# A gated mix of linear attention and an S4D convolution: running sums by accumulating transfers in pairs of rows, one to two iterations apart

## The chip, the cores and the metric

The kernel runs on one core of a Trainium2 chip. The metric is device time in microseconds (us): the median of several runs. The core has five engines with a program each, which run in order and meet at semaphores: TensorE (PE, its weight loads listed as PEld), VectorE (DVE), ScalarE (ACT), GpSimd (POOL) and SyncE (SP). SP and POOL also issue transfers (DMA); POOL issues those that accumulate into their destination. All data are 32-bit floats; matmuls run on a rounded high part and a low part of each operand so as to keep precision.

## The reference, cut to what matters

```python
g = sigmoid((x * gate_w).sum(-1, keepdims=True))           # x: 1 x 2048 x 448
a = attention(x, wqkv, wo)
b = s4d(x, log_A_real, A_imag, C_real, C_imag, log_dt, D_skip)
return g * a + (1 - g) * b

def attention(x, wqkv, wo):                                # 16 heads of 28
    q, k, v = split(x @ wqkv)
    phi = lambda t: where(t > 0, t + 1, exp(t)) + 1e-6
    kv  = einsum("bhsd,bhse->bhde", phi(k), v)
    z   = einsum("bhsd->bhd", phi(k))
    o   = einsum("bhqd,bhde->bhqe", phi(q), kv) / (einsum("bhqd,bhd->bhq", phi(q), z) + 1e-6)
    return merge(o) @ wo

def s4d(u, ...):                                           # K from A, C and dt, then a causal convolution
    return irfft(rfft(u, 2L) * rfft(K, 2L))[:L] + u * D_skip
```

## The kernel before

The 2048 rows of `x` are cut into NC = 16 chunks of 128 rows (one row on each partition), and the chunks into four groups of G = 4. Row `p` of a group's partition dimension holds four consecutive positions, one in each of its four chunks.

For parameters like these the convolution's kernel is constant to the precision needed apart from its first tap, so that the convolution is a running sum of `x` along the sequence, times a factor per channel (`near`). A second routine, `general_conv`, stands behind a test of the parameters and does not run here. The running sum of a group is made in three stages:

- Inside a partition over its four rows: `group_load` (L422, a transfer that SP issues) brings the four chunks into the group's `homes[g]`, then two transfers that accumulate, both `running` (L427, issued by POOL), add shifted rows. Step 1 adds rows 0 to 2, read from HBM, to rows 1 to 3; step 2 adds rows 0 and 1 of the result to rows 2 and 3, inside SBUF. Step 2 may not start before step 1 has landed, and POOL waits for that where step 2 stands in its program.
- Across partitions: `group_split` takes the group's last row into a high part (ACT, L431) and a low part (POOL, L242, tile `sums`), and `group_heads` multiplies both by a triangle of ones on TensorE (L438).
- `convolve` (L443 and L444, DVE) adds the heads to two of the four rows at a time and multiplies by `near`. Then `group_add` (L450) is another accumulating transfer, from `homes[g]` into `y`, and the last row's values go to `u` (L447, SP).

The main loop (L503 to L562) runs over chunks 2 to 13. One pass c projects K of chunk c + 1 (`project`, 11 matmuls, L340), projects q of chunk c (11 matmuls) and accumulates the outer product of `xn` and `phi(k)` of chunk c into four PSUM banks (`do_g`, 11 matmuls, L415). `split_t` prepares the turned chunk c + 2 for TensorE: ACT copies the high part and POOL subtracts it for the low part (`xt`, L246 and L242); `split_n` does so for the plain chunk (`xn`, L252 and L242) and also starts `y` with `x * D_skip` (L258, POOL). `k_feature`, `k_high` and `k_low` make `phi(k)` on ACT and DVE (L366 to L378), `q_post` makes `phi(q)` (L386 to L393) and keeps it in `pq`. The q projection has one PSUM bank, so that q of the next chunk waits until L393 has read the last one.

The order on each engine is that of the code: the schedule is written out by hand, as positions in the loop. `group_load` of group g stands in pass 2g + 2, step 1 at that pass's end, step 2 in the middle of pass 2g + 3 (behind `split_t`), `group_split` in pass 2g + 4, `group_heads` in pass 2g + 5, and `convolve` in passes 2g + 6 and 2g + 7.

The homes are `spare`, half of the weights' tile `wvo` (whose real contents, `wo`, come in pass 10), the last four chunks of `pq` (whose real contents come from pass 12 on; the first loads put the S4D parameters there, and `s4d_prepare` reads them in the first passes), and `spare` again for the last group.

Behind the loop the matrices of attention and output projection are multiplied together, and for each chunk `norm_a` to `norm_d` (POOL and DVE) divide q by its denominator, `turn` transposes it and `attend` (11 matmuls, L660) makes the output rows, which `final_b` mixes with `y` and sends out.

## Time and profile before

| | |
|---|---|
| median of 3 runs | 199.99 us (198.42 to 200.40) |
| the profiled execution | 200.24 us |
| its span, first to last instruction | 198.5 us |
| mean granted TensorE clock | 0.953 |
| busy: PE / PEld / DVE / ACT / POOL | 170.5 / 149.9 / 134.3 / 106.1 / 120.0 us |
| transfers: SP's queue / POOL's queue | 21.81 MB / 8.26 MB |
| mean rate of the transfers | 153 GB/s |

The profile is of one execution; its times are counted from the start of its span. In a row of the instructions in order of time stand: start, length, engine, line, operation, output and inputs, shapes, how many like it were merged, and in brackets the idle time of the engine ahead of it with what ended that. A matmul's length reaches over the start of the next, since they are pipelined. Instructions on POOL that follow a transfer's issue are likewise shown with lengths that overlap the next. A row of waits gives the engine, the waiting tile and its line, what it waited for, the total in us, the number of times and the longest. The main loop lies between about 22 and 138 us.

### The profile page before, as it was taken

To read this page: it belongs to the slowest core of one execution; us is meant where nothing else is said; L and a number is where in the kernel's file an instruction comes from. 1 tells how busy PE (TensorE), PEld (TensorE's weight loads), DVE (VectorE), ACT (ScalarE), POOL (GpSimd) and SP (SyncE) were. 2 spreads that over 40 slices of the span, in tenths; PEclk is the share of its full clock that TensorE was granted. 3 is DMA by queue.
4 is the path that set the end of the run, shared out by engine and by line. 5 is a ranking of instruction groups with operands and counts; after the bars stand their busy time and mean duration, and the time that the engine had idled before them with its cause. 6 is when DMAs were issued, how large, how long until landed. Compare 5 with 4: busy or idle time off the path is not lost.

```text
span 198.5 us, 2704 instructions
## 1 busy us (share of the span) xinstructions
PE 170.5 (86%) x852; PEld 149.9 (76%) x852; DVE 134.3 (68%) x232; ACT 106.1 (53%) x241; POOL 120.0 (60%) x128
## 2 busy tenths in 40 slices
PE   7999999860499879952997988997999999999991
PEld 2798999750498769931896867995897999999990
DVE  0758566710498167997561888878789798997550
ACT  3787788700526195317453645974746466455531
POOL 5246588205970991880519946798597799774200
PEclk9999999997579999996699999999999999999998
DMA  6999683995978409896588799109003122222212
GB/s 199 417 291 266 186 299 117 301 242 131 289 234 146 92 2 139 198 185 225 105 209 160 139 257 225 59 0 185 1 1 63 48 93 93 92 94 96 93 65 82
DMA packets 12186, 30.37 MB, mean 153 GB/s; under 512 B 1549, under 2 KB 7898, under 8 KB 12170
## 3 DMA queue, kind: packets, MB, share of 16 engines
q1 hardware_dynamic: 9274, 21.81, 33.5%
q0 software_dynamic: 2752, 8.26, 23.2%
q8 instruction: 7, 0.11, 0.3%
q10 hardware_dynamic: 144, 0.11, 0.2%
q14 instruction: 9, 0.07, 0.1%
HBM read 20.68 MB, written 3.67 MB: 123 GB/s over the span
## 4 chain that ended last, share of the span: by engine, by line
PE 38%; DMA 28%; DVE 10%; POOL 9%; ACT 8%; issue 5%; ACTq 0%; POOLq 0%; SPq 0%
PE a L660 18%; DMA spare<-in 13%; DMA wvo<-in 5%; DMA pq<-in 4%; PE g L415 4%; PE tr L634 4%; POOL y L258 3%; PE v L340 3%; DMA y<-spare 3%; POOL xn L242 3%; PE q L264 2%; PE q L340 2%; DVE pq L444 2%; DVE spare L444 2%; DMA spare<-spare 2%
## 5 line engine op out<-in xcount | busy, mean ns | idle before, releaser
L340 PE MATMUL q<-wqh,xt 128*128 128x450 f32 x120 | 29.9, 388 | 8.2 <-DVE pq L393 8.2
L660 PE MATMUL a<-wk,th 128*128 128x448 f32 (+1 forms) x170 | 36.7, 361 | 0.1
L415 PE MATMUL g<-pkh,xn 128*128 128x448 f32 x112 | 35.9, 366 | 0.0
L340 PEld LDWEIGHTS q<-wqh,xt 128*128 128x128 f32 x120 | 23.6, 202 | 11.8 <-DVE pq L393 9.7
L660 PEld LDWEIGHTS a<-wk,th 128*128 128x128 f32 x170 | 29.4, 189 | 2.4 <-ACT th L645 0.4
L340 PE MATMUL k<-wk,xt 128*128 128x448 f32 x77 | 20.4, 404 | 11.7 <-POOL xt L242 11.7
L242 POOL TENSOR_TENSOR xt<-xr,xt 128x512 fp32r<-128x512 f32 x14 | 23.7, 1696 | 8.6 <-ACT xt L246 8.6
L340 PEld LDWEIGHTS k<-wk,xt 128*128 128x128 f32 x77 | 15.4, 207 | 14.8 <-POOL xt L242 13.2
L242 POOL TENSOR_TENSOR xn<-xr,xn 128x448 fp32r<-128x448 f32 x16 | 23.5, 1471 | 4.5 <-ACT xn L252 4.4
L415 PE MATMUL g<-pkl,xn 128*128 128x448 f32 x64 | 23.5, 367 | 0.0
L415 PEld LDWEIGHTS g<-pkh,xn 128*128 128x128 f32 x112 | 21.2, 189 | 2.3
L340 PE MATMUL v<-wk,xt 128*128 128x448 f32 x99 | 21.6, 364 | 0.9 <-POOL xt L242 0.9
L258 POOL TENSOR_TENSOR y<-xr,rows 128x448 f32<-128x448 f32 x16 | 22.3, 1393 | 0.0
L572 POOL TENSOR_TENSOR prod<-pq,zb 128x448 f32<-128x448 f32 x16 | 18.6, 1172 | 3.6 <-ACT zb L694 2.6
L340 PEld LDWEIGHTS v<-wk,xt 128*128 128x128 f32 x99 | 18.5, 188 | 2.5 <-POOL xt L242 1.3
L597 POOL TENSOR_TENSOR pn<-pq,den 128x336 f32<-128x336 f32 x16 | 12.3, 768 | 7.5 <-ACT den L586 5.3
L665 DVE SCALAR_TENSOR_TENSOR ot<-y,og,a 128x448 f32<-128x448 f32 (+1 forms) x17 | 10.7, 629 | 5.5 <-PE a L660 5.5
L378 DVE SCALAR_TENSOR_TENSOR pkl<-v,pkh 128x448 fp32r<-128x448 f32 x9 | 5.6, 619 | 13.1 <-ACT pkh L372 13.0
L642 DVE TENSOR_TENSOR th<-tr,th 128x512 fp32r<-128x512 f32 x16 | 11.0, 691 | 2.7 <-ACT th L641 2.1
L378 DVE SCALAR_TENSOR_TENSOR zb<-v,zb 128x448 f32<-128x448 f32 x9 | 5.6, 620 | 10.2 <-ACT pkh L372 10.2
L415 PEld LDWEIGHTS g<-pkl,xn 128*128 128x128 f32 x64 | 11.3, 177 | 1.3 <-DVE pkl L378 0.2
L340 PE MATMUL q<-wql,xt 128*128 128x450 f32 x45 | 12.2, 379 | 0.0
(171 smaller groups left out, 334.6 us busy)
## 6 DMA issues: line engine op xcount, KB each, us to landing
xr<-in SPq DMA_DIRECT2D x15, 512.0 KB, 5.0
out<-ot SPq DMA_DIRECT2D x15, 224.0 KB, 1.9
pq<-in SPq DMA_DIRECT2D x4, 448.0 KB, 13.0
spare<-in SPq DMA_DIRECT2D x2, 896.0 KB
wvo<-in SPq DMA_DIRECT2D x2, 896.0 KB, 11.9
y<-spare POOLq DMA_DIRECT2D x2, 896.0 KB, 6.6
spare<-in POOLq DMA_DIRECT2D x2, 672.0 KB, 10.4
y<-in SPq DMA_DIRECT2D x2, 480.0 KB, 3.8
```

Source lines behind the costliest of these rows:

```text
L242: eng.tensor_tensor(out=o, in0=r, in1=h.bitcast(F32), op=ALU.subtract)
L258: POOL.tensor_tensor(out=y[:, c], in0=plain[c][:, :D], in1=dsk, op=ALU.mult)
L340: PE.matmul(o[:, :n], lhsT=a, rhs=b, start=run.n == 1, stop=not seq)
L378: DVE.scalar_tensor_tensor(out=o, in0=pk, scalar=1e-6, in1=a, op0=ALU.add, op1=op)
L415: PE.matmul(g[i][:a.shape[1], :D], lhsT=a, rhs=b, start=c == 0 and n == 0, stop=c == NC - 1 and n == len(seq) - 1)
L444: DVE.tensor_tensor(out=a, in0=a, in1=near[:, None, :].to_broadcast(full), op=ALU.mult)
L572: POOL.tensor_tensor(out=pd[c], in0=pq[:, c], in1=zb, op=ALU.mult)
L597: POOL.tensor_tensor(out=n[:, :3, :DJ].rearrange("p j (h d) -> p j h d", h=4), in0=a, in1=r[:, :H - 4].rearrange("p (j h) -> p j h", j=3)[ ...
L634: PE.transpose(o[:, j * P:(j + 1) * P], n[:, j], ident)
L642: DVE.tensor_tensor(out=l, in0=ov, in1=h.bitcast(F32), op=ALU.subtract)
L660: PE.matmul(a[:, lo:hi], lhsT=u_, rhs=w_[:, lo:hi], start=n == 0, stop=n == 10)
L665: DVE.scalar_tensor_tensor(out=ot[:, lo:hi], in0=y[:, c, lo:hi], scalar=og[:, c:c + 1], in1=a[:, lo:hi], op0=ALU.mult, op1=ALU.add)
```

## The change

Only the first stage of the running sum and its places change, with the homes.

`running` becomes two steps of another form, both inside SBUF and both over two rows. `running_a` adds row 0 to row 1 and row 2 to row 3 in one transfer. `running_b` adds row 1 to rows 2 and 3, with row 1 read twice. Step b has to wait until a has landed; a has to wait until the group's load has landed. The rows read again from HBM in the old step 1 (672 KB for each group) are no longer read; both new steps move 448 KB.

A table, `pieces_at`, gives the pass in which each step is issued, always behind `split_t`. Loads are in passes 2, 4, 5 and 7 (before: 2, 4, 6, 8), steps a in 3, 5, 6 and 8, steps b in 4, 6, 8 and 10, splits in 5, 7, 9 and 11 (before: 4, 6, 8, 10). Heads, `convolve` and `group_add` keep their passes.

A new tile `room` is the home of the third group. The first group's home is now `wvo`, the second's the end of `pq`, the fourth's `spare`, so that none is used twice. `room` is as large as the tiles `prod` (three slots) and `pn` (two slots) of the part behind the loop, which now live in it; `zl` moves to the slot of `sums`.

```diff
+    room = const.tile([P, 2 * NAT + 3 * D], F32, name="room")
...
-    homes = (spare, wvo[:, 1], pq[:, NC - G:], spare)
+    homes = (wvo[:, 1], pq[:, NC - G:], room[:, :G * D].rearrange("p (r d) -> p r d", r=G), spare)
...
-    def running(g, step):
+    def running_a(g):
         w = homes[g]
-        src = xin[g * G:(g + 1) * G - 1, :, NAT:LO].rearrange("r p d -> p r d") if step == 1 else w[:, :G - step]
-        POOL.dma_start(out=w[:, step:], in_=src, accum_op=ALU.add)
+        POOL.dma_start(out=w[:, 1::2], in_=w[:, 0::2], accum_op=ALU.add)
+
+    def running_b(g):
+        w = homes[g]
+        POOL.dma_start(out=w[:, 2:], in_=w[:, 1:2].to_broadcast([P, 2, D]), accum_op=ALU.add)
...
+    pieces_at = {3: [(running_a, 0)], 4: [(running_b, 0)], 5: [(running_a, 1)], 6: [(running_b, 1), (running_a, 2)],
+                 8: [(running_b, 2), (running_a, 3)], 10: [(running_b, 3)]}
...
-        if c in (2, 4, 6, 8):
-            group_load(c // 2 - 1)
+        if c in (2, 4, 5, 7):
+            group_load(c // 2 - (c < 5))
...
-        if c in (3, 5, 7, 9):
-            running(c // 2 - 1, 2)
+        for f, k in pieces_at.get(c, ()):
+            f(k)
...
-        if c in (4, 6, 8, 10):
+        if c in (5, 7, 9, 11):
             group_split(c // 2 - 2)
...
-        if c in (2, 4, 6, 8):
-            running(c // 2 - 1, 1)
...
-        pd[c] = tp.tile([P, D], F32, name="prod", tag="pk", bufs=3)
+        pd[c] = room[:, 2 * NAT + c % 3 * D:][:, :D]
...
-        n = pn[c] = tp.tile([P, J, P], F32, name="pn", tag="pn")
+        n = pn[c] = room[:, c % 2 * NAT:][:, :NAT].rearrange("p (j t) -> p j t", j=J)
...
-    zl = tp.tile([P, D], F32R, name="zl", tag="pk", bufs=3)
+    zl = tp.tile([P, D], F32R, name="zl", tag="v0", bufs=1)
```

How POOL's program changes is seen around the first group. Before, from the end of pass 2 (L427 is a step of the running sum, `y<-xr,rows` is `y`'s start, `xt`, `xn` and `sums` are low parts):

```order
L427 DMA spare<-in 128x3x448
L242 TENSOR_TENSOR xt<-xr,xt 128x512
L427 DMA spare<-spare 128x896
L258 TENSOR_TENSOR y<-xr,rows 128x448
L242 TENSOR_TENSOR xn<-xr,xn 128x448
L258 TENSOR_TENSOR y<-xr,rows 128x448
L242 TENSOR_TENSOR xt<-xr,xt 128x512
L242 TENSOR_TENSOR sums<-spare,sums 128x448
```

After, from pass 3 on, where the lines are counted by the new file (L427 is step a, L431 step b, L243 and L259 are the former L242 and L258):

```order
L243 TENSOR_TENSOR xt<-xr,xt 128x512
L427 DMA wvo<-wvo 128x2x448
L259 TENSOR_TENSOR y<-xr,rows 128x448
L243 TENSOR_TENSOR xn<-xr,xn 128x448
L259 TENSOR_TENSOR y<-xr,rows 128x448
L243 TENSOR_TENSOR xt<-xr,xt 128x512
L431 DMA wvo<-wvo 128x2x448
L243 TENSOR_TENSOR xn<-xr,xn 128x448
L259 TENSOR_TENSOR y<-xr,rows 128x448
L243 TENSOR_TENSOR xt<-xr,xt 128x512
L427 DMA pq<-pq 128x2x448
L243 TENSOR_TENSOR sums<-wvo,sums 128x448
```

One `xt` stood between the two steps of the first group; now there are four low parts and starts of `y` between them, and the first step of the second group stands ahead of the first group's `sums`.

On SP, behind the load of the weights into `wvo`, the loads of chunks (`xr`), of groups and the rows of `u` stood so before (L422 is a group's load, L447 a row of `u`):

```order
L422 DMA wvo<-in 128x4x448
L206 DMA xr<-in 128x1024 x2
L422 DMA pq<-in 128x4x448
L206 DMA xr<-in 128x1024
L447 DMA u<-spare 1x16x28 x2
L535 DMA okr<-oks 1x112x1
L206 DMA xr<-in 128x1024
L422 DMA spare<-in 128x4x448
```

and now (L423 is a group's load, L451 a row of `u`):

```order
L423 DMA pq<-in 128x4x448
L207 DMA xr<-in 128x1024
L423 DMA room<-in 128x4x448
L207 DMA xr<-in 128x1024 x2
L423 DMA spare<-in 128x4x448
L451 DMA u<-wvo 1x16x28 x2
L541 DMA okr<-oks 1x112x1
L207 DMA xr<-in 128x1024 x2
```

All group loads now stand ahead of the first rows of `u`; before, the last one stood behind them.

## The prediction

> **What bounds the kernel now.** I read the waits first, then TensorE's instructions in order of time with the idle time ahead of them, then POOL and DVE over the same stretch. In the waits (engine, tile and line, what it waited for, us in total, times, longest) the transfers of the running sums stand out:
>
> ```profile
> POOL spare L427 <- DMA spare<-in: 22.5, 3, 10.5
> ACT sums L431 <- DMA wvo<-wvo: 4.0, 1, 4.0
> POOL wvo L427 <- DMA wvo<-in: 6.6, 1, 6.6
> POOL pq L427 <- DMA pq<-in: 4.8, 1, 4.8
> ```
>
> POOL stands still for 22.5 + 6.6 + 4.8 = 33.9 us because L427 issues the second step of a group's running sum and must first see the first step landed. POOL works in order, so everything behind L427 waits too, among it the low halves `xt` (L242) that TensorE's next K projection needs. What that costs is read on TensorE (start, length, operation, count, idle time before it and its releaser):
>
> ```profile
> 36.27 2.27 PE L340 MATMUL v<-wk,xt 128*128 128x448 f32 x10 [0.88 <-POOL xt L242]
> 42.79 0.36 PE L340 MATMUL k<-wk,xt 128*128 128x448 f32 x1
> 52.18 4.10 PE L340 MATMUL k<-wk,xt 128*128 128x448 f32 x10 [9.03 <-POOL xt L242]
> 56.08 2.17 PE L340 MATMUL q<-wqh,xt 128*128 128x450 f32 x8
> ...
> 69.48 2.27 PE L340 MATMUL k<-wk,xt 128*128 128x448 f32 x10 [0.63 <-POOL xt L242]
> 72.84 1.89 PE L340 MATMUL q<-wqh,xt 128*128 128x450 f32 x8 [1.08 <-DVE pq L393]
> ...
> 85.46 2.27 PE L340 MATMUL k<-wk,xt 128*128 128x448 f32 x10 [0.68 <-POOL xt L242]
> 93.21 3.37 PE L340 MATMUL q<-wqh,xt 128*128 128x450 f32 x8 [5.47 <-DVE pq L393]
> 96.38 1.33 PE L340 MATMUL q<-wql,xt 128*128 128x450 f32 x3
> ...
> 108.72 2.28 PE L340 MATMUL k<-wk,xt 128*128 128x448 f32 x10 [1.34 <-POOL xt L242]
> ...
> 119.94 1.89 PE L340 MATMUL q<-wqh,xt 128*128 128x450 f32 x8 [1.68 <-DVE pq L393]
> ...
> 124.48 2.37 PE L340 MATMUL k<-wk,xt 128*128 128x448 f32 x11
> 126.68 1.77 PE L340 MATMUL q<-wqh,xt 128*128 128x450 f32 x8
> 128.29 0.76 PE L340 MATMUL q<-wql,xt 128*128 128x450 f32 x3
> ...
> 131.09 2.37 PE L340 MATMUL v<-wk,xt 128*128 128x448 f32 x11
> ```
>
> The gaps between 35 and 120 us sum to 0.88 + 9.03 + 0.63 + 1.08 + 0.68 + 5.47 + 1.34 + 1.68 = 20.8 us. Behind the two long ones the same matmuls run slower: 10 in 4.10 instead of 2.27 us and 8 in 2.17 instead of 1.77 after the first (2.2 us lost), 8 in 3.37 and 3 in 1.33 instead of 1.77 and 0.76 after the second (2.2 us). The page's row of the granted clock dips at just these places:
>
> ```profile
> PEclk9999999997579999996699999999999999999998
> ```
>
> The Trainium skill (TensorE: Matmul & The Clock Gate, Part 1) says that about one idle window of some 3.4 us takes the clock to half until the array has been busy for as long; the trace agrees, since gaps of 5.47 and 9.03 us were followed by slow matmuls and gaps up to 1.68 us were not.
>
> So 20.8 + 4.4 = 25.2 us of this stretch is TensorE waiting or running slow. Undisturbed, an iteration takes 131.09 - 124.48 = 6.61 us on it. The stretch behind the loop has nothing to give: TensorE is busy for all of 160 to 180 us.
>
> ```profile
> 160.00:180.00 20.00, 20.00 (x115) 18.48 (x114) 18.24 (x45) 11.76 (x30) 17.42 (x25) 1.00 0.23 88
> ```
>
> **The waits that go.** POOL's record around the first and the third group, with a quiet `y` and `xt` ahead for their price:
>
> ```profile
> 25.55 1.16 POOL L258 TENSOR_TENSOR y<-xr,rows 128x448 f32<-128x448 f32 x1
> 26.67 1.29 POOL L242 TENSOR_TENSOR xt<-xr,xt 128x512 fp32r<-128x512 f32 x1
> ...
> 33.46 1.44 POOL L427 DMA_DIRECT2D spare<-in  x1
> 34.42 1.79 POOL L242 TENSOR_TENSOR xt<-xr,xt 128x512 fp32r<-128x512 f32 x1
> ...
> 80.07 0.91 POOL L427 DMA_DIRECT2D pq<-pq  x1 [4.77 <-DMA pq<-in]
> ...
> 86.96 1.74 POOL L242 TENSOR_TENSOR sums<-pq,sums 128x448 fp32r<-128x448 f32 x1
> ```
>
> Before, the dependent second step stands one `xt` behind the first. Afterwards `running_a` and `running_b` of a group are one iteration apart (two for groups 2 and 3), so about 6.6 us of other work lies between issue and wait. Their landing times, from the view of transfers (KB, us from issue to landing; the 12.9 is the first group's, in the window 20 to 34 us):
>
> ```profile
> spare<-spare POOLq DMA_DIRECT2D x2, 448.0 KB, 4.3
> pq<-pq POOLq DMA_DIRECT2D x1, 448.0 KB, 4.8
> pq<-in POOLq DMA_DIRECT2D x1, 672.0 KB, 7.4
> spare<-in POOLq DMA_DIRECT2D x1, 672.0 KB, 12.9
> ```
>
> Both new steps move 448 KB inside SBUF. The trace has no such transfer in rows of 448 elements, only contiguous ones of that size (4.3 and 4.8 us) and three-row ones from HBM (7.4 with little beside it, 12.9 amid loads). I take 5 to 7, nearest the first kind, with 4.3 and 12.9 as ends. All these waits on L427, and the five gaps that name `xt` (0.88 + 9.03 + 0.63 + 0.68 + 1.34 = 12.6 us), go, with 2.2 us of slow clock. POOL issues eight such transfers before and after; each holds it for at most the 0.96 us between 33.46 and 34.42, so that is no change. The fourth group also no longer waits for the first one's `y` addition to free its home.
>
> The other three gaps, 1.08 + 5.47 + 1.68 = 8.2 us and 2.2 of slow clock, come through DVE. The 1.08 follows ACT's wait of 4.0 us for the second step (L431 on `wvo`) and goes with it. The long ones are these:
>
> ```profile
> 80.80 8.87 DVE L444 TENSOR_TENSOR wvo<-wvo,rows 128x896 f32<-128x896 f32 x1
> 111.93 4.46 DVE L444 TENSOR_TENSOR pq<-pq,rows 128x896 f32<-128x896 f32 x1
> 120.92 2.08 DVE L444 TENSOR_TENSOR spare<-spare,rows 128x896 f32<-128x896 f32 x1
> ```
>
> The 8.87 us one ends at 89.67, 0.97 us after POOL's unbroken run from 80.07 ended at 86.96 + 1.74 = 88.70: it got through only when POOL stopped. That run is POOL catching up after its wait. 8.87 led to the gap of 5.47, 4.46 to that of 1.68, and 2.08 to none. With POOL no longer late, the long runs shorten, but they do not vanish: iterations 6, 8 and 10 now put one or two transfers between `xt` and `xn`, in the very place where L444 asks for its turn. Two transfers, `xn` and `y` are 2 x 0.96 + 2 x 1.16 = 4.2 us, about what made the 4.46. I charge two of the three with 1.25 us each, 2.5 in all; ends are 0 and, for one of the old size, 5.47 + 2.2.
>
> The Trainium skill (SBUF — State Buffer, Who interferes with whom) says that a DVE instruction with two SBUF inputs shares a read port with GpSimd, locked for one whole instruction. By that rule alone L444 would lose one POOL instruction, 1.3 us or so, the 2.5 us would be nought and the forecast 177.5 instead of 180.0; here it lost a whole run of 8.6 us, so the measurement decides.
>
> **What the change adds.** `group_split` moves one iteration later, into the same iteration as `group_heads`. In POOL's order shown with the change, `sums` (the low half that the heads need) stood five instructions behind the second step, with an iteration of TensorE still ahead of the heads. Now another group's step a, which waits for that group's load, stands ahead of `sums`, and the heads follow in the same iteration.
>
> The first group is the tight one. POOL's `xt` moves up to 33.46, step a issues at 33.46 + 1.29 = 34.8; with 0.96 for it, 3 x 1.16 and 1.29 for the work behind, step b follows at 40.5, or when a has landed (34.8 + 5 to 7), so at 40.5 to 42. Landed at 45.5 to 49. Then ACT's copy and POOL's low half, from these:
>
> ```profile
> 51.17 0.57 ACT L431 CAST sums<-spare 128x448 fp32r<-128x448 f32 x1 [11.43 <-DMA spare<-spare]
> 51.81 1.42 POOL L242 TENSOR_TENSOR sums<-spare,sums 128x448 fp32r<-128x448 f32 x1
> ```
>
> 0.57 + 1.42 = 2.0, so ready at 47.5 to 51. TensorE starts that iteration at 42.79 - 0.88 = 41.9 and comes to the heads at its end, 6.61 later, at 48.5. Wait: 0 to 2.5 us; I take 1.5. If b lands only after 12.9 us it is 8.4.
>
> For groups 1 to 3 the time from step b to the split is a period plus ACT's way from its `xt` copy to the end of the second K exponential, less `xt` on POOL:
>
> ```profile
> 126.68 0.62 ACT L246 CAST xt<-xr 128x512 fp32r<-128x512 f32 x1
> ...
> 128.29 0.58 ACT L367 ACTIVATE e<-e 128x448 f32<-128x448 f32 x1
> ```
>
> 6.61 + (128.87 - 126.68) - 0.62 - 1.29 = 6.9 us against a landing of 5 to 7, or 7.4: nearly hidden. I charge 1.0 for the three together (0 to 18). Without that cover the whole landing would fall on ACT, and `pkh` and the `q` exponentials are queued behind it.
>
> On SP the loads of groups 1 to 3 (L422) change home and place, as its order shows: all three now stand ahead of the first `u` rows. The one into `pq` overwrites the parameters that the S4D preparation reads, the last time here:
>
> ```profile
> 37.85 0.69 DVE L298 SCALAR_TENSOR_TENSOR y<-pq 112x512 f32<-112x512 f32 x1
> ```
>
> It goes out at 38.5 at the earliest; its step a comes behind step b of the first group, after 40.5, an `xn`, a `y` and an `xt`, so at 45 or later. Behind it on SP is an `x` load that was itself held back before, by POOL's wait. No cost.
>
> The new tile `room` also carries `prod` and `pn` in the tail, with as many slots as before (three and two); its group's `y` addition is issued in iteration 11, far ahead of the first `norm_a`. `zl` shares a slot with `sums`, last read in iteration 11. Both cost nothing unless that addition landed over ten us late.
>
> **The sum.** 25.2 - 1.5 - 2.5 - 1.0 = 20.2 us off the span of 198.5, so 178.3. The profiled execution took 200.24 us, 1.74 outside its span, and stands 0.25 over the median of 199.99. 178.3 + 1.74 = 180.0; the 0.25 is within the spread of the runs, so I forecast 180.0.
>
> **Rivals.** *POOL's runs still shut out L444.* For it: the 8.87, and more transfers in mid-iteration. Against: POOL's run then was a backlog from a wait that goes. One hit of the old size in place of a charge of 1.25: 180.0 + 7.6 - 1.25 = 186.4; two: 192.8. Chance 0.15.
>
> *The loads crowd each other.* With a home for each group, loads that waited for an earlier group now go out early, beside the `x` loads. Two 896 KB loads issued together took
>
> ```profile
> wvo<-in SPq DMA_DIRECT2D x2, 896.0 KB, 11.9
> ```
>
> A step a that waits 5 us longer for its load, with `sums` behind it, would hold the heads for up to that: 185. Against it: in SP's order each `x` load still stands ahead of the next group's load. Chance 0.12.
>
> *Slower: the chain load, a, b, split, heads is too short.* Should every b land in L us, TensorE waits L - 4.5 for the first group (42 + L + 2.0 against 48.5) and at most L - 6.9 for each other, with 2.2 of slow clock behind each. 4L - 25.2 + 8.8 passes the 25.2 gained by 2 us at L = 10.9. At 12.9 it is 35.2, thus 198.5 - 25.2 + 35.2 + 1.74 = 210.2. For it: that 12.9 was measured. Against: its source was HBM and it was 672 KB; those inside SBUF took 4.3 to 4.8. Chance 0.04.
>
> *It does not do what it says:* the waits only move to L431, with the same sum, 200. The iteration between speaks against it. Chance 0.03.
>
> **The numbers.** The forecast has 0.66, with its own range from the floor, 198.5 - 25.2 + 1.74 = 175.0, to 184 (heads at 2.5, 1.5 from the others and 5 from L444). The range 175.5 to 188 adds the crowded loads and one old-size hit, leaving out the rest, under 0.2. About 1% is what a measurement of this kernel can tell from no change. Faster by over 1%: 0.66 + 0.15 + 0.12 = 0.93; same 0.03; slower 0.04.
>
> **What would show it.** Right: no wait of POOL on a first step over 3 us, TensorE's gaps before 115 us under 6 us together and no dip in its clock, iterations near 6.7 us. The heads of the first group should show a gap of 0 to 2.5 behind `sums`. L444 at 4 to 5 us in two of iterations 6, 8 and 10 bears out the 2.5; at 8 the first rival. It would be wrong if step b landed in over 9 us, or ACT stood before `sums` for over 3 us in each group.

## The result, and the profile after

| | before | after |
|---|---|---|
| median of 4 runs | 199.22 us (198.42 to 200.40) | 184.48 us (181.43 to 186.07) |
| the profiled execution | 200.24 us | 185.1 us |
| its span | 198.5 us | 183.2 us |
| mean granted TensorE clock | 0.953 | 0.987 |
| transfers, all queues | 30.37 MB | 29.45 MB |

The ratio is 0.916, with a 95% interval from 0.902 to 0.931. It is lower than the ratio of the two medians, because a ratio leaves out runs more than 1.5% above the fastest of the same kernel: here two of the four of the changed kernel, among them the profiled one, and further down, among others, one of 276 us (the homes alone) and one of 580 us (the operand in PSUM). In a second series the same kernel took 186.17 us (185.46 to 186.5) against 199.33, a ratio of 0.934 (0.931 to 0.938), and its profile shows the same two longest gaps on TensorE. The change makes the kernel about 7 to 8% faster; the forecast was 180.0 us.

The lines of the changed file are L427 for step a, L431 for step b, L435 for ACT's copy into `sums`, L243 for POOL's low parts (`sums`, `xt`, `xn`), L442 for the heads, L448 for the second instruction of `convolve` and L454 for `group_add`.

The page's row of the granted clock of after has one dip in the main loop, where before had two deep ones:

```profile
PEclk9999999999996999999999999999999999999998
```

TensorE of after in order of time, with the idle time ahead of an instruction in brackets. These are all the gaps between 35 and 120 us, with the projection behind the longest one:

```profile
45.75 1.85 PE L341 MATMUL q<-wqh,xt 128*128 128x450 f32 x8 [1.77 <-DVE pq L360]
...
56.06 1.12 PE L442 MATMUL v<-sums,tri 128*128 128x448 f32 x2 [5.23 <-ACT rows L321]
56.97 3.32 PE L341 MATMUL v<-wk,xt 128*128 128x448 f32 x11
...
74.71 1.88 PE L341 MATMUL q<-wqh,xt 128*128 128x450 f32 x8 [0.70 <-DVE pq L394]
...
86.26 0.47 PE L442 MATMUL v<-sums,tri 128*128 128x448 f32 x1 [0.59 <-ACT sums L435]
87.47 0.47 PE L442 MATMUL v<-sums,tri 128*128 128x448 f32 x1 [0.75 <-POOL sums L243]
...
98.21 1.87 PE L341 MATMUL q<-wqh,xt 128*128 128x450 f32 x8 [1.04 <-DVE pq L394]
...
103.62 0.47 PE L442 MATMUL v<-sums,tri 128*128 128x448 f32 x1 [0.93 <-POOL sums L243]
```

Before, five of eight gaps named `xt`, and none does now. The gaps sum to 1.77 + 5.23 + 0.70 + 0.59 + 0.75 + 1.04 + 0.93 = 11.0 us. Behind the longest, the 11 matmuls of `v` take 3.32 us instead of the usual 2.37 and the two of the heads 1.12 us instead of 0.67 (the row is shown with the run without steps), so the slow clock takes another 1.4. Together 12.4 us, against 25.2 before.

The releaser named at 56.06, `rows` (L321), is a copy that stands in ACT's program behind the one into `sums` (L435) and was late with it. The waits show for what:

```profile
ACT sums L435 <- DMA wvo<-wvo: 8.1, 1, 8.1
...
ACT sums L435 <- DMA room<-room: 2.6, 1, 2.6
...
POOL wvo L431 <- DMA wvo<-wvo: 2.1, 1, 2.1
```

POOL's waits on a first step have shrunk from 33.9 us to 2.1. In their place ACT stands 8.1 us before the copy into the first group's `sums`, until that group's step b has landed. The chain of waits gives the two steps of that group (start, us from issue to landing):

```profile
34.71 7.74 DMA wvo<-wvo
42.75 11.27 DMA wvo<-wvo
```

The gap of 1.77 us has another origin. DVE and POOL of after around the first group's step a:

```profile
35.66 5.59 DVE L299 SCALAR_TENSOR_TENSOR y<-pq 112x512 f32<-112x512 f32 x1
...
41.29 0.69 DVE L299 SCALAR_TENSOR_TENSOR y<-pq 112x512 f32<-112x512 f32 x1
...
66.20 4.96 DVE L448 TENSOR_TENSOR wvo<-wvo,rows 128x896 f32<-128x896 f32 x1
...
90.52 4.13 DVE L448 TENSOR_TENSOR room<-room,rows 128x896 f32<-128x896 f32 x1
```

```profile
34.71 1.33 POOL L427 DMA_DIRECT2D wvo<-wvo  x1
35.63 1.61 POOL L259 TENSOR_TENSOR y<-xr,rows 128x448 f32<-128x448 f32 x1
37.03 1.32 POOL L243 TENSOR_TENSOR xn<-xr,xn 128x448 fp32r<-128x448 f32 x1
38.14 1.30 POOL L259 TENSOR_TENSOR y<-xr,rows 128x448 f32<-128x448 f32 x1
39.25 1.44 POOL L243 TENSOR_TENSOR xt<-xr,xt 128x512 fp32r<-128x512 f32 x1
42.75 1.21 POOL L431 DMA_DIRECT2D wvo<-wvo  x1 [2.06 <-DMA wvo<-wvo]
```

The S4D preparation's reading at L299 takes 0.69 us, and 5.59 us right behind the issue of step a. It ends at 41.25, 0.56 us after POOL's unbroken run from 34.71 ended at 39.25 + 1.44 = 40.69. That is the picture of L444 in the profile of before, at a place where it had not been. The K feature, on which the next q projection waits through L360, comes behind it on DVE. The second series shows the same at L299 (5.58 us). For L448 only the 4.1 us of pass 10 returned there; in pass 7, where POOL had paused for 0.41 us just before, it took 1.15.

### The profile page after: what moved, and what is told of

Same layout as the page of the kernel before. It is cut to its first block, busy times and chain, and to the rows that moved or that the text cites. A ratio compares the mean times of both kernels' runs of the same rounds, so it can differ in the third digit from the quotient of the medians.

```text
span 183.2 us, 2706 instructions
## 1 busy us (share of the span) xinstructions
PE 166.5 (91%) x852; PEld 147.8 (81%) x852; DVE 130.4 (71%) x232; ACT 105.9 (58%) x241; POOL 123.2 (67%) x128
## 2 busy tenths in 40 slices
DMA packets 12186, 29.45 MB, mean 161 GB/s; under 512 B 1549, under 2 KB 8410, under 8 KB 12170
## 3 DMA queue, kind: packets, MB, share of 16 engines
HBM read 17.93 MB, written 3.67 MB: 118 GB/s over the span
## 4 chain that ended last, share of the span: by engine, by line
PE 51%; DMA 20%; DVE 8%; ACT 8%; POOL 6%; issue 2%; SPq 1%; ACTq 0%; DVEq 0%; POOLq 0%
PE a L664 20%; DMA wvo<-wvo 10%; PE g L416 8%; PE v L341 7%; PE q L341 6%; DMA room<-room 5%; PE tr L638 4%; PE k L341 3%; DVE wvo L448 3%; DMA wvo<-in 3%; DVE room L448 2%; POOL xt L243 2%; DMA y<-in 2%; POOL y L259 2%; POOL xn L243 2%
## 5 line engine op out<-in xcount | busy, mean ns | idle before, releaser
L341 PE MATMUL q<-wqh,xt 128*128 128x450 f32 x120 | 27.8, 368 | 3.5 <-DVE pq L360 1.8
L243 POOL TENSOR_TENSOR xt<-xr,xt 128x512 fp32r<-128x512 f32 x14 | 21.2, 1515 | 14.2 <-ACT xt L247 14.2
L243 POOL TENSOR_TENSOR xn<-xr,xn 128x448 fp32r<-128x448 f32 x16 | 23.9, 1492 | 5.7 <-ACT xn L253 3.9
L341 PEld LDWEIGHTS q<-wqh,xt 128*128 128x128 f32 x120 | 22.3, 188 | 6.2 <-DVE pq L394 2.5
L259 POOL TENSOR_TENSOR y<-xr,rows 128x448 f32<-128x448 f32 x16 | 21.8, 1365 | 0.0
L576 POOL TENSOR_TENSOR room<-pq,zb 128x448 f32<-128x448 f32 x16 | 18.6, 1168 | 3.6 <-issue 2.6
L341 PEld LDWEIGHTS v<-wk,xt 128*128 128x128 f32 x99 | 19.5, 197 | 1.5
L341 PE MATMUL k<-wk,xt 128*128 128x448 f32 x77 | 17.4, 368 | 0.1
L601 POOL TENSOR_TENSOR room<-pq,den 128x336 f32<-128x336 f32 x16 | 12.2, 763 | 7.4 <-ACT den L590 4.4
L341 PEld LDWEIGHTS k<-wk,xt 128*128 128x128 f32 x77 | 14.3, 187 | 1.8 <-ACT wk L464 0.4
L645 ACT CAST th<-tr 128x512 fp32r<-128x512 f32 x16 | 9.4, 588 | 4.6 <-PE tr L638 4.4
L373 ACT ACTIVATE pkh<-v 128x448 fp32r<-128x448 f32 x9 | 4.9, 543 | 12.3 <-DVE v L369 12.3
```

The lines of the kernel that those rows point to most:

```text
L243: eng.tensor_tensor(out=o, in0=r, in1=h.bitcast(F32), op=ALU.subtract)
L259: POOL.tensor_tensor(out=y[:, c], in0=plain[c][:, :D], in1=dsk, op=ALU.mult)
L341: PE.matmul(o[:, :n], lhsT=a, rhs=b, start=run.n == 1, stop=not seq)
L576: POOL.tensor_tensor(out=pd[c], in0=pq[:, c], in1=zb, op=ALU.mult)
L601: POOL.tensor_tensor(out=n[:, :3, :DJ].rearrange("p j (h d) -> p j h d", h=4), in0=a, in1=r[:, :H - 4].rearrange("p (j h) -> p j h", j=3)[ ...
L645: ACT.copy(h, ov)
```

## The experiments

The theory that the prediction leaves standing: the gain comes from the passes in which the steps are issued, because POOL no longer waits for its own first step. What is missing of it has two causes. A transfer that POOL issues ahead of other work shuts out DVE until POOL pauses (the shut-out), and a step lands late beside other transfers (the crowding). The rivals: that the new form or the homes bring the gain; that a step is slow whatever is beside it; that the rest of the idle time has nothing to do with the steps.

### What brings the gain

The changed kernel once more, unaltered, as a baseline of its own series:

> The changed kernel unaltered, as the measure for the kernels timed beside it. Both theories: between 181 and 186 us, as in its first timing.

It took 186.17 us, with gaps of 1.77 us ahead of the q projection and 5.04 us ahead of the first heads.

Then the old form of the steps in the new passes and homes:

```diff
     def running_a(g):
         w = homes[g]
-        POOL.dma_start(out=w[:, 1::2], in_=w[:, 0::2], accum_op=ALU.add)
+        src = xin[g * G:(g + 1) * G - 1, :, NAT:LO].rearrange("r p d -> p r d")
+        POOL.dma_start(out=w[:, 1:], in_=src, accum_op=ALU.add)
...
-        POOL.dma_start(out=w[:, 2:], in_=w[:, 1:2].to_broadcast([P, 2, D]), accum_op=ALU.add)
+        POOL.dma_start(out=w[:, 2:], in_=w[:, :2], accum_op=ALU.add)
```

> The changed kernel with the old form of the steps (step a adds three rows from HBM, 672 KB; step b adds two contiguous rows, 448 KB) in the new passes and homes. If the places bring the gain and not the form, the time is within 3 us of 186 (slower for the 0.7 MB more from HBM in a stretch whose queues are full). If the form brings it, the time is above 192.

186.09 us, ratio 0.932 (0.927 to 0.937): the same as the changed kernel in the second series. TensorE's two gaps stand where they stood:

```profile
45.95 1.86 PE L341 MATMUL q<-wqh,xt 128*128 128x450 f32 x8 [1.85 <-DVE pq L360]
...
56.54 1.11 PE L443 MATMUL v<-sums,tri 128*128 128x448 f32 x2 [4.79 <-ACT rows L321]
```

POOL's waits on a first step come to 5.1 us in this run, against 33.9 in the kernel before. So pairs of rows, and the 2.75 MB less that are read from HBM, bring nothing measurable here.

The homes alone, in the kernel before (each group has its own; form and passes as before):

```diff
-    homes = (spare, wvo[:, 1], pq[:, NC - G:], spare)
+    homes = (room[:, :G * D].rearrange("p (r d) -> p r d", r=G), wvo[:, 1], pq[:, NC - G:], spare)
```

> The kernel before with only a home for each group added (group 0 in the new tile); steps, form and passes as before. What the prediction says of the parts: the homes take away the wait of 6.5 us on the fourth group's load and what follows it (gap of 1.34, half of the 1.68), 2 to 3 us: 196 to 197.5. Rival: the homes alone let the loads go out early and the rest comes with that: under 190.

200.46 us, ratio 1.004 (1.000 to 1.008): no gain. What the fourth group's home gives is lost one group earlier, where DVE's second instruction of `convolve` (L445 in that file) is now shut out and a third slow stretch follows on TensorE:

```profile
101.87 7.84 DVE L445 TENSOR_TENSOR pq<-pq,rows 128x896 f32<-128x896 f32 x1
```

```profile
113.25 3.31 PE L341 MATMUL q<-wqh,xt 128*128 128x450 f32 x8 [3.33 <-DVE pq L394]
```

With neither the form nor the homes bringing anything by themselves, the passes are what is left. They weren't run alone, since steps so far apart need homes that are free for longer; that the gain is theirs is concluded from the two runs above.

### What the steps still cost

The changed kernel without steps a and b, everything else in place. The running sums inside a group are then left out, so its output is another:

```diff
-    pieces_at = {3: [(running_a, 0)], 4: [(running_b, 0)], 5: [(running_a, 1)], 6: [(running_b, 1), (running_a, 2)],
-                 8: [(running_b, 2), (running_a, 3)], 10: [(running_b, 3)]}
+    pieces_at = {}
```

> Both steps of all groups left out (so the running sums inside a partition are missing from the output); loads, splits, heads and additions stay. All theories: ACT waits for no landing before sums, the heads have no gap over 0.5 us. 'Crowding' and 'shut-out' together say that the steps' landing and POOL's issues of them account for the larger part of the 12.5 us that TensorE still loses: time 174 to 177. If only the placement of loads counted, it would stay above 180.

172.27 us, ratio 0.865 (0.862 to 0.869), with a span of 169.9 us. TensorE has one gap of over 0.3 us in the loop, and DVE's instructions of the same two places are short:

```profile
49.52 0.67 PE L442 MATMUL v<-sums,tri 128*128 128x448 f32 x2 [0.49 <-ACT rows L321]
```

```profile
35.67 0.92 DVE L299 SCALAR_TENSOR_TENSOR y<-pq 112x512 f32<-112x512 f32 x1
...
58.30 1.15 DVE L448 TENSOR_TENSOR wvo<-wvo,rows 128x896 f32<-128x896 f32 x1
...
79.00 1.90 DVE L448 TENSOR_TENSOR room<-room,rows 128x896 f32<-128x896 f32 x1
```

L299 takes 0.92 us instead of 5.59. Is that only because POOL has more pauses without the steps? L448 of pass 6 answers it. It stands at 51.86 and takes 1.42 us, in the middle of a run in which POOL does not pause:

```profile
50.05 1.17 POOL L243 TENSOR_TENSOR xn<-xr,xn 128x448 fp32r<-128x448 f32 x1 [3.11 <-PE v L442]
51.17 1.16 POOL L259 TENSOR_TENSOR y<-xr,rows 128x448 f32<-128x448 f32 x1
52.28 2.15 POOL L243 TENSOR_TENSOR xt<-xr,xt 128x512 fp32r<-128x512 f32 x1
54.39 1.16 POOL L243 TENSOR_TENSOR xn<-xr,xn 128x448 fp32r<-128x448 f32 x1
```

It got its turn when the `y` at 51.17 ended, and POOL's next instruction waited for it (2.15 us instead of 1.29). Here, without a transfer ahead, the two engines took turns, one instruction each. Behind a transfer they don't: in after, POOL's instructions follow its issue at 34.71 with lengths that overlap by 0.19 to 0.21 us (35.63 + 1.61 = 37.24 against the next start at 37.03), here by 0.04 to 0.05 (50.05 + 1.17 against 51.17), and DVE isn't let in until the run is over. A short pause is enough: behind the `y` addition that POOL issues at 103.50 in after it is idle for 0.19 us, and the next L448 takes 1.15 us; in the run with early loads below it follows the same addition without a pause, and L448 takes 3.63.

Eight transfers of 448 KB thus cost 186.17 - 172.27 = 13.9 us in the changed kernel, and nearly all that is left of idle time in the loop comes from them.

### Do the loads make the steps late?

Loads of groups 2 and 3 later, in passes 7 and 8 (steps a of these groups in passes 7 and 9, so that they stand behind their loads):

```diff
+    pieces_at = {3: [(running_a, 0)], 4: [(running_b, 0)], 5: [(running_a, 1)], 6: [(running_b, 1)],
+                 7: [(running_a, 2)], 8: [(running_b, 2)], 9: [(running_a, 3)], 10: [(running_b, 3)]}
...
-        if c in (2, 4, 5, 7):
-            group_load(c // 2 - (c < 5))
+        if c in (2, 4, 7, 8):
+            group_load({2: 0, 4: 1, 7: 2, 8: 3}[c])
```

> Loads of groups 2 and 3 in passes 7 and 8 instead of 5 and 7, their steps a in 7 and 9, their steps b still in 8 and 10. Theory 'crowding': step b of group 0 landed 11.3 us after its issue because 3.8 MB of loads went out within 5 us of it; with 1.8 MB of them gone it lands in 6 to 8.5 us, TensorE's gap ahead of the first heads falls from 5.2 to under 2.5 us, its clock does not dip, and the time falls by 3 to 5 us. Rival 'form': a step of two rows of 448, one of them read twice, is slow by itself; then it still takes about 11 us and the time stays within 1 us. Rival 'shut-out of DVE': the loads were late because DVE was kept from the S4D parameters until 41.9 us; that is not touched here, and by this theory alone the gain is under 2 us.

188.1 us (183.5 to 188.75; they spread too far for a ratio). ACT waited 8.8 us for the first group's step b, not less than 8.1. A miss.

The other direction, loads of groups 1 to 3 in passes 3 and 4 and the weights for `wo` in pass 9 instead of pass 4:

```diff
-        if c == 4:
+        if c == 9:
             SP.dma_start(out=wvo[:, 0], in_=wvo_d[:, 0])
...
-        if c in (2, 4, 5, 7):
-            group_load(c // 2 - (c < 5))
+        for k in {2: (0,), 3: (2,), 4: (3, 1)}.get(c, ()):
+            group_load(k)
```

> Same steps in the same passes; only SP's order of loads: group 2's behind x of pass 3 (about 27 us), group 3's in the place of the value weights (about 34 us), the value weights in pass 9. So 1.8 MB fewer are queued on SP between 42 and 54 us, where step b of group 0 is under way (2.5 instead of 4.3 MB). Theory 'crowding', sharpened by the late loads (0.9 MB fewer, landing unchanged): while SP's queue is backed up, a step gets about 50 GB/s whatever its length; SP's queue now empties at about 51 us, so that b lands in 8 to 10 instead of 11 us, the gap ahead of the first heads falls from 5.0 to 2 to 4 us and the time by 1 to 4. Rival 'shut-out of DVE' alone: b lands as late as before, since the loads still go out at 42 us; time within 1 us of 186.

186.93 us, ratio 0.938 (0.932 to 0.943), and again 8.2 us of ACT's waiting. Another miss: between 34 and 60 us 5.53 MB moved instead of 6.95, but the DMA engines were still busy from 45 us on, for the whole flight of step b. From 42 to 54 us SP's queue moved 2.48 MB here and 2.49 with the late loads, as much as in after (2.46). These two runs moved loads and left as many beside step b; they don't tell crowding from a step that is slow by itself. The last run below does.

### Does POOL's run shut out DVE?

L299 out of the way of step a, by doing the whole reading one pass earlier:

```diff
-            steps(2 if c == 4 else 1)
+            steps({2: 2, 3: 0, 4: 2}[c])
```

> The whole reading of the S4D parameters in pass 2 instead of half in pass 2 and half in pass 3. Theory 'shut-out of DVE': in pass 3 one DVE instruction on them lasted 5.59 instead of 0.69 us while POOL worked without a pause; moved to pass 2 it lasts about 0.7, K's feature of the next chunk is 4 us earlier and TensorE's gap of 1.77 us at 45.75 goes; the loads of groups 1 to 3 go out from about 34.5 instead of 42.1 us, so that step b of group 0, still waiting for its step a, meets fewer of them: landing 7 to 10 us and 2 to 4 us of time gained. Rival 'crowding': the same loads now meet step a instead of step b, and it lands later than 7.7 us; the heads of the first group stay as late and only the 1.77 us go.

187.59 us, ratio 0.940 (0.936 to 0.944): no gain. The next instruction of the kind behind step a takes the place of L299, here the TENSOR_SCALAR of the q feature, which takes 0.38 us when left alone:

```profile
36.89 5.74 DVE L357 TENSOR_SCALAR t<-e 128x448 f32<-128x448 f32 x1
```

```profile
43.51 3.34 PE L341 MATMUL q<-wqh,xt 128*128 128x450 f32 x8 [4.62 <-DVE tri L538]
```

The gap ahead of the first heads is gone in this run (ACT waited 0.6 us), but 1.46 and 4.62 us stand earlier. Step b landed at 54.6, no earlier than in after (54.0): TensorE, held up before, only came later.

Step a of the first group earlier, at the end of pass 2, ahead of `xt` instead of behind it:

```diff
-    pieces_at = {3: [(running_a, 0)], 4: [(running_b, 0)], ...
+    pieces_at = {4: [(running_b, 0)], ...
...
+        if c == 2:
+            running_a(0)
```

> Step a of group 0 issued at the end of pass 2, ahead of the xt of pass 3 instead of behind it; nothing else. Theory 'shut-out of DVE': POOL's run behind the issue is then xt and y only and ends at about 36.8 when POOL waits for ACT's xn; the DVE instruction on the S4D parameters lasts 1 to 3 instead of 5.6 us, TensorE's gap of 1.77 us goes, the loads start 3 to 4 us earlier, and step b goes out at about 40.5 instead of 43 and lands by 49 to 52 instead of 54. Time 181 to 184 against 186. Rival 'crowding' alone: step a meets the same queue (value weights and x), b meets the earlier loads, the first heads stay 4 to 5 us late; time within 1 us of 186.

186.36 us, ratio 0.932 (0.926 to 0.938). Ahead of the first heads there are 0.40 us instead of 5.2, but step b again landed at 53.5, and the shut-out has moved, and its gap with it:

```profile
34.65 6.32 DVE L357 TENSOR_SCALAR t<-e 128x448 f32<-128x448 f32 x1
```

```profile
41.85 3.17 PE L341 MATMUL q<-wqh,xt 128*128 128x450 f32 x8 [3.30 <-DVE pq L360]
```

What makes an instruction a victim? L448 reads two operands from SBUF, the sums and `near`. Here its second operand lies in PSUM; it multiplies by the heads instead of by `near`, so the result is another and the work is the same:

```diff
-        DVE.tensor_tensor(out=a, in0=a, in1=near[:, None, :].to_broadcast(full), op=ALU.mult)
+        DVE.tensor_tensor(out=a, in0=a, in1=heads[g][:, None, :].to_broadcast(full), op=ALU.mult)
```

> The changed kernel with DVE's multiplication by near replaced by one by the heads in PSUM (the product is then another; times count): it has one SBUF operand instead of two, as the addition ahead of it has. Theory 'shut-out': it takes 1.08 us in every pass, in pass 10 too (4.1 before), TensorE's gaps of 0.3 to 1 us from DVE's pq after it go, and the time falls by 1 to 3 us against 186; the 5.6 us on the S4D parameters stay. Rival: POOL's run does not matter to it and it stays at 4 us in pass 10.

184.29 us, ratio 0.919 (0.914 to 0.925), some 2 us less than the changed kernel in its second series. L448 takes 1.09 us in all eight passes, with the same transfers beside it, while L299 is shut out as before:

```profile
36.17 5.57 DVE L299 SCALAR_TENSOR_TENSOR y<-pq 112x512 f32<-112x512 f32 x1
...
87.55 1.09 DVE L448 TENSOR_TENSOR room<-room,v 128x896 f32<-128x896 f32 x1
```

The same place, pass 10, in the changed kernel of the second series:

```profile
88.09 4.14 DVE L448 TENSOR_TENSOR room<-room,rows 128x896 f32<-128x896 f32 x1
```

In both, POOL has issued a step 0.3 us before and follows it with `xn` and `y` without a pause. So the second operand in SBUF is what exposes L448: 4.1 us with it, 1.09 without. The 2 us of time can't be put down to it, since TensorE's gap behind L448 was only 0.32 us in the second series, and the 184.48 us of the first series lie as low. The Trainium skill (SBUF — State Buffer, Who interferes with whom) says that a DVE instruction contends with GpSimd when both its inputs lie in SBUF and the GpSimd instruction reads SBUF, or when it runs in a two-port mode, which a TENSOR_SCALAR can enter; the victims L448, L299 and L357 agree. It also says that whoever comes first holds the ports for one whole instruction. The run without steps agrees (1.42 us in mid-run); behind a transfer the measurement differs, 5.59 us and four instructions of POOL behind one issue.

### Better places

Three attempts to use both findings. First, everything of the first group earlier: its load ahead of the loop, step a in pass 2, step b at the end of pass 3:

```diff
+    group_load(0)
...
+    pieces_at = {2: [(running_a, 0)], 5: [(running_a, 1)], 6: [(running_b, 1), (running_a, 2)],
+                 8: [(running_b, 2), (running_a, 3)], 10: [(running_b, 3)]}
...
+        if c == 3:
+            running_b(0)
```

> Only the first group is moved: its load ahead of the loop (about 14 us), its step a in pass 2 behind xt (about 28 us), its step b at the end of pass 3 (about 38 to 40 us); the loads of the other groups, the forms and the later steps as in the changed kernel. Theory 'the first group is too late': its b, issued before SP's queue is backed up with the loads of 42 to 48 us, lands by 47; ACT's wait of 8 us before sums and TensorE's gap of 5 us at the first heads go, its clock does not dip there, and the time falls by 5 to 7 us, from 186 to 179 to 181. Also no transfer is issued ahead of DVE's reading of the S4D parameters in pass 3, so that instruction should take 0.7 to 2 instead of 5.6 us and the gap of 1.77 go with it. Rival 'the whole stretch is bound by transfers': the wait moves to the second group, and the gain is under 2 us.

184.14 us, ratio 0.918 (0.915 to 0.922). Step b went out at 44.3 instead of 38 to 40 and landed at 55.2, where by 47 was expected. The gap ahead of the first heads falls to 0.57 us, but each issue finds a victim at its new place, and each of them makes a gap:

```profile
29.57 7.05 DVE L299 SCALAR_TENSOR_TENSOR y<-pq 112x512 f32<-112x512 f32 x1
...
45.85 4.85 DVE L357 TENSOR_SCALAR t<-e 128x448 f32<-128x448 f32 x1
```

```profile
40.85 3.27 PE L341 MATMUL q<-wqh,xt 128*128 128x450 f32 x8 [3.20 <-DVE pq L360]
...
51.58 1.87 PE L341 MATMUL q<-wqh,xt 128*128 128x450 f32 x8 [2.45 <-DVE sm L288]
```

It is the fastest of the three. Its interval lies below that of the changed kernel in the second series, but inside that of the first, so it isn't claimed to be a gain.

Second, all steps at the ends of passes, one to a pass, with loads, `u` and weights moved to suit:

```diff
+    ends_at = {3: [(running_b, 0)], 4: [(running_a, 1)], 5: [(running_b, 1)], 6: [(running_a, 2)],
+               7: [(running_b, 2)], 8: [(running_a, 3)], 9: [(running_b, 3)]}
...
+        if c == 2:
+            running_a(0)
...
+        for f, k in ends_at.get(c, ()):
+            f(k)
```

> All at once: the first group as in the other kernel; every later step a or b at the end of a pass (a in 4, 6, 8, b in 5, 7, 9) instead of between xt and xn, b ahead of the group addition; loads of groups 2 and 3 in passes 6 and 7; the value weights in pass 9; the rows of u in passes 9, 10 and 12, so that SP's loads of x do not wait behind them. Theory: no step stands between xt and xn, so DVE's multiplication by near is not shut out in pass 10 (1 to 2 instead of 4.1 us) and b always has more than a pass to land; the time nears that without any steps, 172.3: 174 to 177. Rival 'transfers bind': ACT still waits 2 us or more before sums of some group: 178 to 181.

188.79 us, ratio 0.936 (0.930 to 0.942): no better than the changed kernel. A step at the end of a pass runs straight into the next pass's `xt`, `xn` and `y`, which makes POOL's run longer; six DVE instructions of 3.6 to 6.9 us stand in its profile, and three gaps of 3.0 us and more on TensorE.

Last, the first group of the first attempt with step b right behind `xt` in pass 3, where SP's queue is quiet, and the 896 KB of weights moved from pass 4 to pass 9:

```diff
+    pieces_at = {2: [(running_a, 0)], 3: [(running_b, 0)], 5: [(running_a, 1)], 6: [(running_b, 1), (running_a, 2)],
...
-        if c == 4:
+        if c == 9:
             SP.dma_start(out=wvo[:, 0], in_=wvo_d[:, 0])
```

> As the run with the first group's load and step a an iteration earlier (184.14 us), but its step b stands in pass 3 right behind xt, not at that pass's end, and the weights' load moves from pass 4 to pass 9. Theory (what is left is set by where POOL's transfers stand: each is followed by a run of POOL work that shuts out DVE, and a step that meets a full SP queue lands late): step b is issued at about 36 to 41, with a quiet queue lands in 5 to 7 us, no gap ahead of the first heads, the gap of 2.45 us at 51.6 that the 4.85 us TENSOR_SCALAR at L357 caused goes; the 3.20 us at 40.9 behind step a stays: 180.5 to 182.5. Rival (a run of POOL only takes another victim): behind step b the S4D reading at L299 or the TENSOR_SCALAR at L357 takes 4 us or more in pass 3, a gap of 2 us or more follows in place of the old one, and the time stays at 183.5 to 186.

187.0 us, ratio 0.932 (0.930 to 0.935). Neither got the time right. For the first group's step b it went as the theory has it: it landed 4.7 us after its issue, at 40.3, and behind it L357 takes 1.52 us and the two L299 0.68 and 1.52, since POOL pauses soon after. The heads still began at 54.58. Now it is `near` that is late: a small TENSOR_SCALAR of its preparation (L310) takes 2.29 us instead of 0.17 behind the second group's step a, and TensorE waits 1.85 us for the result and 0.48 us ahead of the heads. The transfers in the stretch from 36 to 41 us, where step b is in flight (queue, packets, MB, share; then the issue, KB and us to landing):

```profile
q0 software_dynamic: 272, 0.46, 54.7%
q1 hardware_dynamic: 83, 0.27, 13.5%
...
wvo<-wvo POOLq DMA_DIRECT2D x1, 448.0 KB, 4.7
```

The same step in the changed kernel, 42 to 54 us:

```profile
q1 hardware_dynamic: 1219, 2.46, 63.6%
q0 software_dynamic: 321, 0.54, 25.1%
...
wvo<-wvo POOLq DMA_DIRECT2D x1, 448.0 KB, 11.3
```

The same transfer of 448 KB takes 4.7 us with 0.27 MB of SP's loads beside it, and 11.3 us with 2.46 MB. That settles it for the first group: the step is late because of where it meets the loads. The amount alone doesn't set how late: in the run with the whole S4D reading a pass earlier it landed in 7.4 us with 2.32 MB of SP's loads in the 8 us from 47 on, all queues together at 347 GB/s against 252 in the changed kernel, and why that stretch moved faster is open. The gain was then lost at the place to which the weights had gone. They go out at 74.43, beside the third group's step b at 74.35:

```profile
wvo<-in SPq DMA_DIRECT2D x1, 896.0 KB, 11.2
...
room<-room POOLq DMA_DIRECT2D x1, 448.0 KB, 12.0
```

In the changed kernel that step took 9.6 us. Now ACT waits 4.5 us for it, and TensorE loses 2.89 us ahead of the heads and, with 3.67 instead of 2.37 us for the next 11 matmuls, 1.3 us behind them:

```profile
87.09 0.47 PE L444 MATMUL v<-sums,tri 128*128 128x448 f32 x1 [2.89 <-ACT sums L437]
...
89.31 3.67 PE L341 MATMUL v<-wk,xt 128*128 128x448 f32 x11
```

The Trainium skill (DMA: Bandwidth & Descriptors, Queues, rings and completion order) says that each DMA engine takes turns, packet by packet, between the queues that have work; the traces agree in kind, since 448 KB that has the engines nearly to itself lands in 4.7 us and beside SP's loads in 7.4 to 12.2. SP's loads aren't the only crowd: in after the fourth group's step b took 11.0 us with only 0.63 MB from SP in the 12 us from 90 on, but behind the 896 KB that POOL itself adds into `y` (11.6 us).

## Why the prediction was right or wrong

**The mechanism was right.** POOL's waits on first steps fell from 33.9 to 2.1 us, and the five gaps that named `xt` went, with the slow stretches behind the two long ones. The rival by which the waits only move (200 us) and the slower one (210.2) are out.

**The size was 4.9 us too large:** forecast 20.2 us off the span, measured 198.5 - 183.2 = 15.3. Term by term, what was charged and what it came to:

| term of the sum | charged | measured in after |
|---|---|---|
| heads of the first group | 1.5 (0 to 2.5; 8.4 if b lands after 12.9) | 5.23 + 1.4 slow clock = 6.6 |
| L444 (now L448) shut out | 2.5 | 0.70 + 1.04 = 1.7 |
| heads of groups 1 to 3 | 1.0 | 0.59 + 0.75 + 0.93 = 2.3 |
| L299 shut out | not in the sum | 1.77 |
| sum | 5.0 | 12.4 |

**The step that failed** is "landed at 45.5 to 49" for the first group's step b, because its landing was taken as 5 to 7 us. Both ends of that came from transfers with little beside them; the 12.9 us of the rows amid loads was put aside as a transfer from HBM, and it was the nearer one. Step a landed in 7.74 us and b in 11.27. With these two, the prediction's own working gives the measured time: issued at 42.75, landed at 54.02, plus 2.0 us for the copies, 56.0; the heads start at 56.06 (POOL's copy ended at 55.88, ACT's `rows` behind its own at 56.01). The case "8.4 if b lands only after 12.9 us" was thus nearly what happened. The slow clock of 1.4 us behind it was missing from the charge, though it was in the formula of the slower rival. The 5.23 us and the 1.77 of L299 aren't independent: the landing sets when the heads begin, so that TensorE, without the gap behind L299, would have waited there for as much longer. The runs with the S4D reading or step a earlier bear it out.

**L444 was shut out about as charged:** 4.96 us in pass 7 and 4.13 in pass 10, gaps of 0.7 and 1.0, and in the second series in pass 10 alone, with a gap of 0.32. It was charged in the wrong passes in part (6 and 8 had none of it). The 4.46 us of before, from which the size was taken, were not made as the prediction has it: POOL's run there was `xt`, `xn` and `y` until 115.44, and its last issue stood at 106.13. The parallel in size is luck. What was overlooked is that L444 isn't the only instruction of its kind. The prediction quoted L299 at 0.69 us as "the last time here" when it asked whether the load into `pq` could go out, and didn't ask what the new step a, which POOL issues just then, would do to it: 5.59 us, a gap of 1.77, and a load into `pq` that goes out 3.6 us after the 38.5 that were worked out, as SP of after shows:

```profile
42.06 0.38 SPq L423 DMA_DIRECT2D pq<-in  x1
```

**Groups 1 to 3** came to 2.3 instead of 1.0 us, and within their bounds. Their steps b landed in 4.7, 9.6 and 11.0 us, and the cover of 6.9 us absorbed most of it, as worked out. The rows of 0.75 and 0.93 us are POOL's low half, which comes behind ACT's high half.

**The floor was 2.5 us lower than forecast:** 183.2 - 12.4 = 170.8 against 198.5 - 25.2 = 173.3, and the kernel without steps a and b bears it out with 169.9. Part of it was a gap behind the stretch that was summed, which the prediction didn't look at when it said that there was nothing to gain behind the loop. TensorE of before and of after at that place:

```profile
138.95 0.47 PE L690 MATMUL zo<-zh,ones 128*128 128x448 f32 x1 [1.45 <-ACT zh L688]
```

```profile
123.93 0.47 PE L694 MATMUL zo<-zh,ones 128*128 128x448 f32 x1
```

Of the other 1 us or so, 0.3 us lie behind the rows above, where the rest takes 183.2 - 123.93 = 59.3 us against 198.5 - 138.95 = 59.6; what remains is not accounted for. Each gap is also shown 0.16 us short, since a matmul's row of 0.36 us covers the start of the next, which stands 0.20 us later when nothing holds it; but that holds for the seven gaps of after as for the eight of before, and nearly cancels. Without the lower floor the forecast would have missed by 7.4 us instead of 4.9; that it came as near as it did is in part luck.

**The rivals.** The first (L444 shut out as before) has 186.4 us, closer to the measured 184.5 to 186.2 than the forecast, but by luck: L444 wasn't hit at the old size of 8.87 us, and with L299 the shut-outs came to 1.7 + 1.77 = 3.5 us against 2.5 charged, while the first heads came to 6.6 against 1.5. The second (the loads crowd each other) named the crowding, but put it on step a waiting for its load; in fact the loads held up step b. Its 185 was closest by the time, by another way, which is luck too. The signs named ahead of the result said so: no POOL wait of over 3 us held, but gaps of 11.0 instead of under 6, one dip of the clock and a first step b landing in over 9 us were the marks of a wrong step.

## What to carry to other kernels

A transfer's landing time is read from rows with the same traffic beside them, not from the quietest rows of the same size; here the difference was 4.7 against 11.3 us, and moving a load out of one step's way put it in another's. Where an instruction is shut out by another engine's run, list every instruction that shares the trait (here two operands in SBUF, or a TENSOR_SCALAR inside SBUF), since moving the cause by one place only picks the next victim. Before a stall is moved, a run that leaves its cause out altogether (here 172 us) says how much there is to win, and whether the rest is worth a search.

## What the runs showed of the hardware that was not expected

- Behind a transfer that POOL issues, DVE stays shut out for POOL's whole unbroken run: 5.59 us (L299, ordinarily 0.69), 6.32 and 5.74 (L357, ordinarily 0.38), 7.05 (L299 at another place). Without an issue ahead, an instruction of the same kind gets its turn in mid-run, behind one POOL instruction (1.42 us). The only difference that the rows show is how far POOL's instructions overlap, 0.2 us against 0.05; why an issue does that was not settled.
- An operand in PSUM instead of SBUF took L448 out of this altogether: 1.09 us in eight of eight passes.
- The clock dropped behind gaps of 3.0 us and more, and behind a single one of 2.45 us it did not (8 matmuls in 1.87 us). Two shorter gaps close together are another matter. In six runs one of 1.07 to 2.15 us ahead of a group's heads, with 0.48 to 0.75 us more behind one matmul, was followed by 11 matmuls in 3.22 to 4.31 us instead of 2.37, among them the changed kernel in its second series (1.18 and 0.75 us, then 3.24). In the last run 1.85 and 0.48 us with nine matmuls between them were followed by 3.52 us. The lengths alone don't decide: 1.07 and 0.74 us were followed by 3.50 us in the run with the S4D reading earlier, and by 2.36 in the run with step a earlier.
